# Issuing the later loads of a decode-step kernel from ACT's queue instead of POOL's

## The chip, the cores and the metric

The kernel runs on one core of one Trainium2 chip. A core has five engines with an instruction stream each: PE (matmul), DVE (VectorE), ACT (ScalarE), POOL (GpSimd) and SP (SyncE). Data moves between the device memory (HBM) and the on-chip memory (SBUF) by transfers (DMAs), which an engine issues with a `dma_start` in its own stream and which sixteen DMA engines carry out. A transfer adds to a semaphore sixteen times, once for each DMA engine that is through with its part; it has landed when all sixteen have come. The metric is the device time in microseconds.

## The reference

One decode step with its gradients: a layer norm of `x` (4 x 1 x 512), attention over the last 1024 of 4096 cached positions with 32 query heads on 8 key/value heads, and beside it a gated feed-forward part. The outputs are the result and the gradients by all inputs but one.

```
xn = _layernorm(x)
out = x + _A_ref(xn, k_cache, v_cache, wq, wo) + _B_ref(xn, w_gate, w_up, w_down)
...
W = min(4096, max(256, Sk // 4))                     # 1024
q = (x @ wq) as (B, Hq, Sq, Dh)
k = repeat(k_cache[:, :, Sk - W:, :], 4);  v likewise
p = softmax(q k^T * Dh ** -0.5);  o = p v;  return o @ wo
...
_B_ref: (gelu(x @ w_gate) * (x @ w_up)) @ w_down
```

The gradients by the caches (`out_2`, `out_3`) have the caches' full shape, 33.5 MB each: the last quarter of the positions is computed, the other three quarters are zeros that the kernel has to write.

## The kernel before

**Stages.** First the feed-forward part: `w_down`, `w_gate`, `w_up` are loaded, transposed, multiplied, and the outer products that give their gradients are put in a list `bg` of small pieces. Then comes attention in `NT` = 4 groups (`t` = 0 to 3) of `GP` = 2 key/value heads (`g`). For each group the loop at L766 runs `masks`, `scores(t, 0)` (transposes of K and the scores), `scores(t, 1)` (transposes of V, and the softmax by hooks), `softmax_d`, `pre(t + 1)` (the projections of the next group, with `wo` and `wq`), `odq`, `fin` (the sums that read `wo` and `wq` last), `load_next`, the rest of `bg`, and `dw`, which puts the weight gradients' pieces in `bg`.

**What `scores` does.** Eight steps: for each of the two heads `g` four blocks `q`. A step transposes eight 128 x 128 blocks (L402, `T_ps`, in one of the four buffers of the PSUM pool `ps_w`), copies them with DVE (`T_sb`, L101), multiplies (L407), and then calls `tick`, which takes one or two pieces from `bg`. A piece is a matmul into another buffer of `ps_w` and a copy out of it (`evac`), in most cases by ACT (L99), in some by DVE (L101). The last piece of a tile issues the store, always from SP (`store`, L105).

**The zeros.** `zeros(n)` issues stores of a constant zero tile `ztile` from ACT, 1.5 or 3 MB each (18 in all), in `scores` after block `q == 1` of each head, with numbers by the table `ZN`, and at some other places. `add_manual_dep` ties such a store to the last ACT copy made so far (`last[-1]`): it comes behind that copy in ACT's stream.

**The loads.** `load_w(t)` loads 1 MB of `wo` and 1 MB of `wq`, `load_kv(t, k, g)` 1 MB of K (`kb`, k = 0) or V (`vb`, k = 1). Group 0's, and K and V of group 1's first head, come from SP at the start. All later ones come from POOL: `wo`, `wq`, and K and V of group 1's second head when the feed-forward pools close (L763 to L765), and in `load_next(t)` those of group `t + 2`. There are sixteen of these. K and V have three buffers in `kvp` and one in `wodd`, the weights one in `wres` (even groups) and one in `wodd` (odd groups): a load waits until the group two before has read its tile for the last time. For K and V that is `odq`, for `wo` the sums at the end of `fin`.

**The order.** The order on each engine is fixed when the program is built, by a planner that goes by priority and modelled readiness. So POOL's loads don't stand in the order in which they are written: a V and a K load of group `t + 2` come ahead of the weights.

Of the kernel before, what the change touches and what calls it, by code (L numbers as in the profile page):

```python
# [13 lines left out]
BF16 = mybir.dt.bfloat16  # L14
P = 128
# [3 lines left out]
def kernel(  # L19
# [27 lines left out]
    nc = tc.nc  # L47

    B, Sq, D = A_x.shape
    _, G, Sk, Dh = A_k_cache.shape  # L50
# [4 lines left out]
    K0 = Sk - W  # L55
    F = B_w_gate.shape[1]
    ND = D // P
    NF = F // P
    MB = P // B
    J = W // MB  # L60
    GP = 2
    NT = G // GP
    HG = GP * rep
# [5 lines left out]
    CW = HG * Dh  # L69
# [18 lines left out]
    last = []  # L88
    chain = []

    def evac(out, in_, n, half=False, eng=None):

        eng = "dve" if half else eng or ("act" if chain else None)
        ca, cd = (190 + n) / 1.2, (120 + (n / 2 if half else n)) / 0.96
        if eng is None:
            eng = "act" if load["act"] + ca <= load["dve"] + cd else "dve"
        load[eng] += ca if eng == "act" else cd
        if eng == "act":
            last.append(nc.scalar.copy(out=out, in_=in_))  # L99
            return last[-1]  # L100
        return nc.vector.tensor_copy(out=out, in_=in_)  # L101
# [14 lines left out]
    for c0 in range(0, NF, NF // 2):  # L116
        nc.sync.dma_start(out=wd_sb[:, c0:c0 + NF // 2, :],
                          in_=B_w_down[c0 * P:(c0 + NF // 2) * P, :].rearrange("(c p) n -> p c n", p=P))
# [47 lines left out]
    for b in range(B):  # L166
        nc.vector.tensor_copy(out=sel[:, :, b * rep:(b + 1) * rep],
                              in_=ident_f[:, b * RB:b * RB + 1].unsqueeze(2).broadcast_to([P, 2 * GP, rep]))
# [69 lines left out]
    for src, dstT, adj in ((dy_b, dyT, False), (xn_b, xnT, True)):  # L238
# [4 lines left out]
        if src is dy_b:  # L243
# [3 lines left out]
                                  in_=tps[:].rearrange("p c (b r) -> p c b r", b=B)[:, :, :, 0:8])  # L247
# [22 lines left out]
    wo_v = A_wo.rearrange("(t p k) n -> t p k n", p=P, k=HG)  # L270
    wq_v = A_wq.rearrange("(p c) (t j) -> t p c j", p=P, j=CW)
    wo_t, wq_t, k_t, v_t = {}, {}, {}, {}
# [1 line left out]
    wpool = [wres]  # L274
    kvpool = [kvp] * 3

    def load_w(t):
        eng = nc.gpsimd if t else nc.sync
        pool = wpool[t % 2]
        wo_t[t] = pool.tile([P, HG, D], BF16, name="wo_sb", tag="wo")  # L280
        eng.dma_start(out=wo_t[t][:], in_=wo_v[t])
        wq_t[t] = pool.tile([P, ND, CW], BF16, name="wq_sb", tag="wq")
        eng.dma_start(out=wq_t[t][:], in_=wq_v[t])

    def load_kv(t, k, g):
        d_, src, nm = ((k_t, A_k_cache, "kb"), (v_t, A_v_cache, "vb"))[k]
        tl = kvpool[(GP * t + g) % (2 * GP)].tile([P, J, Dh], BF16, name=nm, tag=nm)
        (nc.gpsimd if GP * t + g > GP else nc.sync).dma_start(out=tl[:].rearrange("p j d -> p (j d)"),
                          in_=src[:, t * GP + g, K0:Sk, :].rearrange("b (m j) d -> m b (j d)", j=J))
        d_[(t, g)] = tl  # L290

    def load_next(t):

        if t + 2 < NT:
            load_w(t + 2)
            for k in range(2):
                for g in range(GP):
                    load_kv(t + 2, k, g)


    zruns = deque([og, 0] for og in (out_2, out_3))
# [21 lines left out]
    def tick(n):  # L323
        for _ in range(min(n, len(bg))):
            bg.popleft()()
# [67 lines left out]
    def scores(t, k, hooks):  # L393

        lf = (qm, dom)[k]
        blks = (k_t, v_t)[k]
        ps = ps_a.tile([P, WQ], FP32, name="S_ps", tag=("S", "dP")[k])
        for g in range(GP):
            for q in range(NQ):
                T_ps = ps_w.tile([P, JQ, P], BF16, name="T_ps", tag="w")  # L400
                for jj in range(JQ):
                    nc.tensor.transpose(T_ps[:, jj, :], blks[(t, g)][:, q * JQ + jj, :], ident[:])  # L402
                T_sb = tsb.tile([P, WQ, B], BF16, name="T_sb", tag="T", bufs=4)
                evac(T_sb[:].rearrange("p n b -> p (n b)"), T_ps[:].rearrange("p j m -> p (j m)"), 1024, half=True)
                s = q * GP + g
                for b in range(B):
                    nc.tensor.matmul(ps[b * RG:(b + 1) * RG, :], lhsT=lf[:, b, s * RG:(s + 1) * RG],  # L407
                                     rhs=T_sb[:, :, b], start=(g == 0 and q == 0),
                                     stop=(g == GP - 1 and q == NQ - 1), tile_position=(0, b * RG))
                for f in hooks.get(g * NQ + q, ()):  # L410
                    f()
                tick(2 if k or q % 2 else 1)
                if q == 1:
                    zeros(ZN[t][GP * k + g])
        st[t][("S", "dP")[k]] = ps[:]
# [195 lines left out]


    NF4 = (NF + 3) // 4
    load_w(0)
    for k in range(2):
        for g in range(GP):
            load_kv(0, k, g)
    for k in range(2):
        load_kv(1, k, 0)
# [106 lines left out]
    for f4 in range(NF4):  # L726
        held = {}
        n = min(4, NF - 4 * f4)
# [30 lines left out]
    with tc.tile_pool(name="stage", bufs=4, reuse_waits="tile") as stage, \  # L759
            tc.tile_pool(name="wodd", bufs=1, reuse_waits="tile") as wodd:  # L760
        wpool.append(wodd)
        kvpool.append(wodd)
        load_w(1)  # L763
        for k in range(2):
            load_kv(1, k, 1)  # L765
        for t in range(NT):  # L766
            if t == 0:
                pre(t, {})
            masks(t)
            scores(t, 0, {})  # L770
            zeros(2 if t == 0 else 0)
            scores(t, 1, softmax(t))
            d1, d2 = softmax_d(t)
            zeros(4 if t == NT - 1 else 0)
            if t + 1 < NT:
                pre(t + 1, {0: [d1], 2: [d2]})
            else:
                tick(2)
                d1()
                tick(6)  # L780
                d2()
                tick(2)
            odq(t)
            fin(t)
            load_next(t)
            tick(len(bg))
            dw(t)
        tick(len(bg))
        zeros(2 * B * G)


        acc_r = kvp.tile([P, 2, ND, B, RB], FP32, name="acc_r", tag="kb")
        nc.vector.tensor_copy(out=acc_r[:], in_=acc[:].unsqueeze(4).broadcast_to([P, 2, ND, B, RB]))
        fin_ps = []
        for o in range(2):
            f_ps = ps_w.tile([P, ND, P], FP32, name="f_ps", tag="w")
            for c in range(ND):
                nc.tensor.transpose(f_ps[:, c, :], acc_r[:, o, c].rearrange("p b r -> p (b r)"), ident_f[:])
            fin_ps.append(f_ps[:])
        acc_o, acc_d = fin_ps[0].rearrange("p c d -> p (c d)"), fin_ps[1].rearrange("p c d -> p d c")  # L800

        def adj(x):
            return x[:].rearrange("p (d c) -> p d c", c=ND)

        out_b = kvp.tile([P, D], BF16, name="out_b", tag="vb")
        nc.vector.tensor_tensor(out=out_b[:], in0=acc_o, in1=x_b[:], op=ALU.add)
        nc.sync.dma_start(out=out_0.rearrange("b s d -> (b s) d"), in_=out_b[0:P:RB, :])

        s1 = const.tile([P, 1], FP32, name="s1")
        nc.vector.reduce_sum(out=s1[:], in_=acc_d, axis=AX.XY)  # L810
        pr = kvp.tile([P, D], FP32, name="pr", tag="vb")
        s2 = const.tile([P, 1], FP32, name="s2")
        nc.vector.tensor_tensor_reduce(out=adj(pr), in0=acc_d, in1=adj(xn_f), scale=1.0, scalar=0.0,
                                       op0=ALU.mult, op1=ALU.add, accum_out=s2[:])
        nm1 = const.tile([P, 1], FP32, name="nm1")
        nc.vector.tensor_scalar(out=nm1[:], in0=s1[:], scalar1=-1.0 / D, scalar2=None, op0=ALU.mult)
        nm2 = const.tile([P, 1], FP32, name="nm2")
        nc.vector.tensor_scalar(out=nm2[:], in0=s2[:], scalar1=-1.0 / D, scalar2=None, op0=ALU.mult)
        nc.vector.scalar_tensor_tensor(out=adj(pr), in0=adj(xn_f), scalar=nm2[:, 0:1], in1=acc_d,
                                       op0=ALU.mult, op1=ALU.add)  # L820
        nc.vector.tensor_scalar(out=pr[:], in0=pr[:], scalar1=nm1[:, 0:1], scalar2=rstd[:, 0:1],
                                op0=ALU.add, op1=ALU.mult)
        dx_b = kvp.tile([P, D], BF16, name="dx_b", tag="kb")
        nc.vector.tensor_tensor(out=dx_b[:], in0=pr[:], in1=dy_b[:], op=ALU.add)
        nc.sync.dma_start(out=out_1.rearrange("b s d -> (b s) d"), in_=dx_b[0:P:RB, :])
# [30 lines left out]
```

## Time and profile before

| | us |
|---|---|
| median of 3 runs | 281.89 (280.82 to 281.97) |
| the profiled execution's own time | 281.41 |
| its span, first to last instruction | 279.6 |

| engine | busy | share of the span | instructions |
|---|---|---|---|
| PE | 212.1 us | 76% | 3126 |
| DVE | 158.7 us | 57% | 336 |
| ACT | 115.0 us | 41% | 214 |
| POOL | 56.0 us | 20% | 56 |

HBM was read for 30.68 MB and written for 81.01 MB. Issues of transfers are not counted in an engine's busy time. In the profile a `q` behind an engine's name (ACTq) is its sequencer, which waits and issues; q1 is the queue that SP's transfers go through, q10 ACT's, q0 POOL's. What POOL issued around the ends of groups 0 and 1:

| issued at, us | transfer | idle before it |
|---|---|---|
| 42.15, 42.89, 43.66, 44.18 | wo, wq, kb, vb of group 1 | 21.31 us for the pieces of the feed-forward part |
| 97.18, 99.63 | vb, kb of group 2 | |
| 104.22, 104.74, 105.49, 106.02 | wo, wq, kb, vb of group 2 | 3.99 us for the sums of `fin` |
| 149.98, 152.44 | vb, kb of group 3 | |
| 156.47, 156.99, 157.75, 158.27 | wo, wq, kb, vb of group 3 | 3.44 us for the sums of `fin` |

### The profile page before, as it was taken

To read this page: it belongs to the slowest core of one execution; us is meant where nothing else is said; L and a number is where in the kernel's file an instruction comes from. 1 tells how busy PE (TensorE), PEld (TensorE's weight loads), DVE (VectorE), ACT (ScalarE), POOL (GpSimd) and SP (SyncE) were. 2 spreads that over 40 slices of the span, in tenths; PEclk is the share of its full clock that TensorE was granted. 3 is DMA by queue.
4 is the path that set the end of the run, shared out by engine and by line. 5 is a ranking of instruction groups with operands and counts; after the bars stand their busy time and mean duration, and the time that the engine had idled before them with its cause. 6 is when DMAs were issued, how large, how long until landed. Compare 5 with 4: busy or idle time off the path is not lost.

```text
span 279.6 us, 7185 instructions
## 1 busy us (share of the span) xinstructions
PE 212.1 (76%) x3126; PEld 137.7 (49%) x3132; DVE 158.7 (57%) x336; ACT 115.0 (41%) x214; POOL 56.0 (20%) x56
## 2 busy tenths in 40 slices
PE   1978976988769879968797978699897775689400
PEld 0856854744435565535465745356664442355200
DVE  6955644546357657654665555477654634376530
ACT  1331643444335246636253544373444442525400
POOL 3890003040200345020007600200520020020000
PEclk9985998699797997999689999999999997597955
DMA  7999999999999999999999999999999999999970
GB/s 236 446 392 430 425 403 392 414 411 423 425 426 422 422 423 416 417 432 423 427 418 350 387 407 430 421 425 421 425 415 431 428 422 423 425 432 421 422 311 22
DMA packets 19423, 112.15 MB, mean 401 GB/s; under 512 B 1456, under 2 KB 5056, under 8 KB 10432
## 3 DMA queue, kind: packets, MB, share of 16 engines
q10 hardware_dynamic: 4400, 50.34, 42.7%
q1 hardware_dynamic: 12304, 44.58, 39.3%
q0 software_dynamic: 2688, 16.78, 15.0%
q8 instruction: 24, 0.39, 0.5%
q14 instruction: 7, 0.06, 0.0%
HBM read 30.68 MB, written 81.01 MB: 399 GB/s over the span
## 4 chain that ended last, share of the span: by engine, by line
PE 52%; DVE 19%; DMA 18%; issue 3%; POOL 2%; ACT 2%; ACTq 0%; DVEq 0%
DMA out_dram<-osb_q 13%; PE T_ps L402 9%; PE kv_ps L540 8%; DVE T_sb L101 6%; PE S_ps L407 6%; DMA out_dram<-osb_g 5%; PE woT_ps L339 3%; PE wgT_ps L745 3%; PE acc_ps L213 2%; PE wqT_ps L598 2%; PE dwo_ps L559 2%; POOL P_x L420 2%; PE od_ps L512 2%; PE dwg_ps L718 2%; PE do_ps L344 2%
## 5 line engine op out<-in xcount | busy, mean ns | idle before, releaser
L101 DVE COPY T_sb<-T_ps 128x1024 bf16<-128x1024 bf16 x64 | 43.8, 690 | 40.1 <-PE T_ps L402 39.6
L99 ACT CAST stg_dv<-kv_ps 128x512 bf16<-128x512 f32 x57 | 30.1, 594 | 33.5 <-PE kv_ps L540 25.8
L99 ACT CAST stg_dk<-kv_ps 128x512 bf16<-128x512 f32 x40 | 22.3, 592 | 36.4 <-PE kv_ps L540 22.8
L540 PE MATMUL kv_ps<-domr,P_x 128*128 128x512 bf16 x63 | 23.4, 439 | 10.5 <-ACT stg_dv L99 5.1
L387 POOL TENSOR_TENSOR domr<-r,msk 128x512 bf16<-128x512 bf16 x8 | 8.2, 1040 | 74.1 <-DVE r L380 74.1
L99 ACT CAST osb_g<-dwg_ps 128x512 bf16<-128x512 f32 (+1 forms) x28 | 14.2, 538 | 19.0 <-PE dwg_ps L718 9.2
L402 PE MATMUL T_ps<-ident,kb 128*128 128x128 bf16 x256 | 21.9, 222 | 0.0
L402 PEld LDWEIGHTS <-kb 128*128 128x128 bf16 x256 | 17.1, 100 | 8.6 <-issue 5.7
L540 PE MATMUL kv_ps<-qmr,dS_x 128*128 128x512 bf16 x60 | 20.9, 432 | 0.5 <-DVE stg_dk L101 0.2
L402 PE MATMUL T_ps<-ident,vb 128*128 128x128 bf16 x256 | 20.8, 223 | 0.1
L99 ACT CAST osb_o<-dwo_ps 128x512 bf16<-128x512 f32 x25 | 14.6, 586 | 12.9 <-PE dwo_ps L559 11.8
L402 PEld LDWEIGHTS <-vb 128*128 128x128 bf16 x256 | 16.2, 100 | 6.9 <-issue 5.0
L407 PE MATMUL S_ps<-T_sb,dom 128*32 128x256 bf16 x128 | 12.7, 387 | 8.3 <-DVE T_sb L101 7.8
L420 POOL TENSOR_TENSOR P_x<-P_b,bmsk 128x1024 bf16<-128x1024 bf16 x4 | 7.6, 1893 | 56.2 <-ACT P_b L468 56.2
L99 ACT CAST osb_q<-dwq_ps 128x512 bf16<-128x512 f32 x25 | 14.1, 589 | 11.1 <-PE dwq_ps L571 6.1
L101 DVE CAST stg_dk<-kv_ps 128x512 bf16<-128x512 f32 x24 | 16.0, 684 | 1.8 <-PE kv_ps L540 1.7
L101 DVE COPY woT<-woT_ps 128x1024 bf16<-128x1024 bf16 x16 | 11.0, 689 | 10.0 <-PE woT_ps L339 10.0
L407 PE MATMUL S_ps<-T_sb,qm 128*32 128x256 bf16 x128 | 13.1, 388 | 4.0 <-DVE T_sb L101 4.0
L339 PE MATMUL woT_ps<-ident,wo_sb 128*128 128x128 bf16 x128 | 12.3, 248 | 2.7 <-DVE stg_dv L101 1.9
L101 DVE COPY wgT<-wgT_ps 128x1024 bf16<-128x1024 bf16 x14 | 9.7, 692 | 7.6 <-PE wgT_ps L745 7.6
L339 PEld LDWEIGHTS <-wo_sb 128*128 128x128 bf16 x128 | 10.4, 113 | 7.2 <-issue 6.4
L101 DVE COPY wqT<-wqT_ps 128x1024 bf16<-128x1024 bf16 x16 | 11.0, 687 | 4.7 <-PE wqT_ps L598 4.6
(214 smaller groups left out, 397.4 us busy)
## 6 DMA issues: line engine op xcount, KB each, us to landing
out_dram<-ztile ACTq DMA_DIRECT2D x14, 3072.0 KB, 22.4
out_dram<-stg_dv SPq DMA_DIRECT2D x8, 1024.0 KB, 25.4
out_dram<-stg_dk SPq DMA_DIRECT2D x8, 1024.0 KB, 17.2
out_dram<-ztile ACTq DMA_DIRECT2D x4, 1536.0 KB, 12.7
kb<-in_A_k_cache_dram POOLq DMA_DIRECT2D x5, 1024.0 KB, 20.0
vb<-in_A_v_cache_dram POOLq DMA_DIRECT2D x5, 1024.0 KB, 24.3
out_dram<-osb_o SPq DMA_DIRECT2D x8, 512.0 KB, 15.8
out_dram<-osb_q SPq DMA_DIRECT2D x8, 512.0 KB, 28.1
```

The costliest lines, as they stand in the source:

```text
L99: last.append(nc.scalar.copy(out=out, in_=in_))
L101: return nc.vector.tensor_copy(out=out, in_=in_)
L213: nc.tensor.matmul(ps[:, c, :], lhsT=lf(c), rhs=rhs, start=(k == 0), stop=(k == len(terms) - 1))
L339: nc.tensor.transpose(wT_ps[:, i, c, :], wo_sb[:, 2 * h2 + i, c * P:(c + 1) * P], ident[:])
L344: nc.tensor.matmul(do_ps[i * RG:(i + 1) * RG, 2 * h2:2 * h2 + 2], lhsT=dyT8[:, c, :], rhs=woT[:, :, c, :].rearrange("p j (g x) -> p j g x" ...
L387: nc.gpsimd.tensor_tensor(out=mr[:, g], in0=st[t]["r4"][:, k, :].unsqueeze(1).broadcast_to([P, NQ, Dh]), in1=msk[:, :, g].unsqueeze(2).bro ...
L402: nc.tensor.transpose(T_ps[:, jj, :], blks[(t, g)][:, q * JQ + jj, :], ident[:])
L407: nc.tensor.matmul(ps[b * RG:(b + 1) * RG, :], lhsT=lf[:, b, s * RG:(s + 1) * RG], rhs=T_sb[:, :, b], start=(g == 0 and q == 0), stop=(g = ...
L420: eng.tensor_tensor(out=dst[:].rearrange("p j (m b) -> p (j m) b", b=B), in0=src[:].unsqueeze(2).broadcast_to([P, WQ, B]), in1=bmsk[:].uns ...
L512: nc.tensor.matmul(od_ps[r0:r0 + rep * B, 0, :], lhsT=pT[:, j % JQ, (j // JQ) * GP + g:P:NS], rhs=blks[(t, g)][:, j, :], start=(j == 0), s ...
L540: nc.tensor.matmul(mps[:].rearrange("p q d -> p (q d)"), lhsT=src[:, jj, :], rhs=mr[:, g].rearrange("p q d -> p (q d)"), start=True, stop= ...
L745: nc.tensor.transpose(wT_ps[:, i, c, :], wsb[:, c, fc * P:(fc + 1) * P], ident[:])
```

## The change

Every load that POOL issued is now issued by ACT. Each is tied to the last ACT copy made so far, as the zeros are. For groups 2 and 3 the two weight tiles are loaded at once in `load_next`, when a group ends. K and V of those groups are put in a list `loads`, as are all four later loads of group 1. `pull(1)` takes one from the list, in `scores(t, 0)`, after the blocks `q` = 0 and 2 of each head: four per group, in the order in which they were put in. For group 1 that is `wo`, `wq`, K, V during group 0's K steps; for groups 2 and 3 the two K and then the two V tiles, during the K steps of groups 1 and 2.

```diff
@@ -274,28 +274,42 @@
-    def load_w(t):
-        eng = nc.gpsimd if t else nc.sync
+    loads = deque()
+
+    def pull(n):
+        for _ in range(min(n, len(loads))):
+            loads.popleft()()
+
+    def fetch(out, in_, first):
+        d = (nc.sync if first else nc.scalar).dma_start(out=out, in_=in_)
+        if not first:
+            tc.add_manual_dep(d.ins, last[-1].ins.name,
+                              mybir.DependencyInfo(mybir.DependencyClass.NoSync, mybir.DependencyReason.DATA))
+
+    def load_w(t, k):
         pool = wpool[t % 2]
-        wo_t[t] = pool.tile([P, HG, D], BF16, name="wo_sb", tag="wo")
-        eng.dma_start(out=wo_t[t][:], in_=wo_v[t])
-        wq_t[t] = pool.tile([P, ND, CW], BF16, name="wq_sb", tag="wq")
-        eng.dma_start(out=wq_t[t][:], in_=wq_v[t])
+        if k == 0:
+            wo_t[t] = pool.tile([P, HG, D], BF16, name="wo_sb", tag="wo")
+            fetch(wo_t[t][:], wo_v[t], t == 0)
+        else:
+            wq_t[t] = pool.tile([P, ND, CW], BF16, name="wq_sb", tag="wq")
+            fetch(wq_t[t][:], wq_v[t], t == 0)
 
     def load_kv(t, k, g):
...
-        (nc.gpsimd if GP * t + g > GP else nc.sync).dma_start(out=tl[:].rearrange("p j d -> p (j d)"),
-                          in_=src[:, t * GP + g, K0:Sk, :].rearrange("b (m j) d -> m b (j d)", j=J))
+        fetch(tl[:].rearrange("p j d -> p (j d)"),
+             src[:, t * GP + g, K0:Sk, :].rearrange("b (m j) d -> m b (j d)", j=J), GP * t + g <= GP)
         d_[(t, g)] = tl
 
     def load_next(t):
 
         if t + 2 < NT:
-            load_w(t + 2)
+            for k in range(2):
+                load_w(t + 2, k)
             for k in range(2):
                 for g in range(GP):
-                    load_kv(t + 2, k, g)
+                    loads.append(lambda k=k, g=g: load_kv(t + 2, k, g))
@@ -410,6 +424,8 @@
                 tick(2 if k or q % 2 else 1)
+                if k == 0 and q % 2 == 0:
+                    pull(1)
                 if q == 1:
                     zeros(ZN[t][GP * k + g])
@@ -760,9 +777,10 @@
-        load_w(1)
         for k in range(2):
-            load_kv(1, k, 1)
+            loads.append(lambda k=k: load_w(1, k))
+        for k in range(2):
+            loads.append(lambda k=k: load_kv(1, k, 1))
```

More of the change, by code (lines that the diff above doesn't have):

```diff
@@ L613 @@
     NF4 = (NF + 3) // 4
-    load_w(0)
+    for k in range(2):
+        load_w(0, k)
     for k in range(2):
@@ L762 @@
         kvpool.append(wodd)
-        load_w(1)
         for k in range(2):
-            load_kv(1, k, 1)
+            loads.append(lambda k=k: load_w(1, k))
+        for k in range(2):
+            loads.append(lambda k=k: load_kv(1, k, 1))
         for t in range(NT):
```

## The prediction

> **What bounds the kernel now.** I read the slices over time first, then the queues.
>
> ```profile
> DMA  7999999999999999999999999999999999999970
> GB/s 236 446 392 430 425 403 392 414 411 423 425 426 422 422 423 416 417 432 423 427 418 350 387 407 430 421 425 421 425 415 431 428 422 423 425 432 421 422 311 22
> ...
> q10 hardware_dynamic: 4400, 50.34, 42.7%
> q1 hardware_dynamic: 12304, 44.58, 39.3%
> q0 software_dynamic: 2688, 16.78, 15.0%
> q8 instruction: 24, 0.39, 0.5%
> ```
>
> The transfers are full from the second slice to the last but two, at about 425 GB/s. 112.15 MB at 425 GB/s is 264 us of the 279.6 us span, while TensorE, the busiest engine, has 76%. So a change of queue pays only through the bytes per second, holes in the stream, or the tail. q0 is POOL's queue: the 16.78 MB that the change moves. q10 is ACT's (the zero stores), q1 is SP's. Next, the same by stretch:
>
> ```profile
> core 0: us, PE busy (x) PEld busy (x) DVE busy (x) ACT busy (x) POOL busy (x), PEclk, DMA share, GB/s
> 138.00:149.00 11.00, 10.58 (x252) 7.15 (x250) 7.61 (x15) 4.74 (x10) 1.00 (x1) 0.82 1.01 420
> 150.00:157.00 7.00, 5.54 (x104) 4.29 (x104) 3.54 (x7) 3.71 (x7) 3.55 (x6) 1.00 0.95 322
> 208.00:256.00 48.00, 35.77 (x462) 20.97 (x461) 25.07 (x48) 19.32 (x38) 3.79 (x2) 0.88 1.01 425
> 272.00:278.00 6.00, 0.00 (x0) 0.00 (x0) 0.00 (x0) 0.00 (x0) 0.00 (x0) 0.50 0.08 33
> ```
>
> Two rows matter. In 272 to 278 the share is 0.08, little more than one of sixteen DMA engines: fifteen are through, one drags out the end. The semaphore records agree: of the sixteen increments of the last osb_q store, half are in by 271.4 us and the last comes at 278.45, **7 us late**. In 150 to 157 only 322 GB/s flow although the engines count as busy; 8192-byte packets of q0 there take 464 ns on average, the usual one 309. For wo's third load (issued 156.5), fourteen increments come by 166.9 us, the last two at 172.2 and 173.8: two engines fell behind on POOL's loads.
>
> The chain of waits shows what the late engine does upstream:
>
> ```profile
> 226.83 35.79 DMA out_dram<-osb_q
> ...
> 262.71 0.59 ACT osb_q L99
> ```
>
> The last is what an ACT-issued transfer can cost, in ACT's timeline:
>
> ```profile
> 233.69 0.61 ACTq L105 DMA_DIRECT2D out_dram<-ztile  x1
> 234.34 1.56 ACT L99 CAST stg_dv<-kv_ps 128x512 bf16<-128x512 f32 x3 [4.38 <-DMA out_dram<-stg_dk]
> ```
>
> A zero store reads a constant tile, yet it waited for a stg_dk store. By its semaphores, SP and ACT draw their transfers from one cycle of eight semaphores, and each waits for the landing of the one eight before it; POOL has eight of its own. The copy behind waited 4.38 us.
>
> **What the Trainium skill says.** "DMA: Bandwidth & Descriptors", section "Issuing engines are not separate DMA queues": all issuers use the same 16 engines, a change of issuer saves only sequencer time. The trace agrees on the whole: a share per MB of 0.85% (q10), 0.88% (q1), 0.89% (q0). The same page, "Latency and other measured facts": two engines (7 and 15) are usually slower, with the descriptor ring of GpSimd's transfers in SBUF as a best guess. Two late engines on POOL's loads fit; the cause isn't shown. "Queues, rings and completion order": each engine takes packets by turns from the queues, and in order within one. That fits the 35.79 us of a 512 KB osb_q store (2048-byte packets against 12288-byte zero packets). It means that loads on ACT's queue stand behind the zeros before them.
>
> **The change part by part.**
>
> *Removed: POOL's issue.* Sixteen transfers at 0.53 to 0.77 us, some 10 us of an engine with 20% busy and waits of 74.1 us for r and 56.2 us for P_b. Worth nothing.
>
> *Added: ACT's issue.* The same sixteen at ACT's own 0.61 us (zero stores): 10 us, ten of them before 157 us (wo, wq, K, V of group 1; wo, wq, two K, two V of group 2). ACT is 41% busy, but its copies free the four ps_w buffers that the transposes need. If a third of the six us of the ten reaches TensorE: +2 us; bounds 0 and +6. The six of group 3 come after 157 us, where 35.79 us of the chain is waiting for a transfer: nothing. The release of wo (last read by acc_sum) doesn't block: it held POOL until 104.22 us, when ACT was idle 2.88 us for a kv_ps anyway.
>
> *Moved: group 1's loads, from 42 us to the K steps at 52 to 64 us.* Zero and FFN stores carry the stream until about 52 us: from 42 to 56.9 us they have some 4.2 MB, 9.9 us at 425 GB/s. Then the loads come one per two K steps. A hole of up to 2 us. In return the osb_d and osb_g stores of 40 to 57 us meet no loads at first and land earlier; ACT waits 7.0 us for osb_g and 2.2 us for osb_d landings. A third of that 9.2 us on the path: -3 us; bounds 0 and -7.
>
> *Moved: K and V of group 3, from 149.98 and 152.44 us to after 157 us.* This is the clear price. In 150 to 157 us, 7 x 322 = 2.25 MB moved, of which 1.02 MB were these two loads by the packet records. The rest is 1.2 MB, 2.9 us at 425: **4.1 us of hole**. Now the same 7 us hold 2.25 / 0.425 = 5.3 us of work, so 1.7 us are lost already. Net +2.4 us. What the stream gains or loses before 150 us is swallowed there, since the queues are nearly dry at 149 us; only the pace of compute shifts it. With +2 and -3 from above: **+1.4 us at 157 us**.
>
> *Order on the queue.* Group 3's last V load stands behind 2 MB of weights, three other MB and 4.6 MB of zeros; 10.7 MB at some 300 GB/s is 36 us from 156 us, landing about 192 us. It lands at 201.36 us now, and is needed about 221 us. No reader waits.
>
> *The eight semaphores.* A group of 51 us now has about 12 SP and ACT transfers; with loads 18. Eight in flight allow 8 x 51 / 18 = 22 us each, and zeros take 22.4 us. Walking the order eight back, I find no binding wait before 150 us and two or three of some 4 us in group 2, in front of a load or a zero store. They hold ACT's copies, then ps_w, then TensorE. The 35.79 us hide them; costed 0, bounds 0 and +6 (if they come before 157 us).
>
> *The late engine.* Between the first transfers and POOL's first (36 to 44 us) the last engine is 1.6 to 3.3 us behind; after POOL's loads 5 to 9, and 7 at the end. Without a software queue I take 3 us: **-4 us**; bounds 0 (it has another cause) and -7 (it goes). What is late next is the fifteen engines themselves, at about 271.5 us.
>
> Sum: 1.4 - 4.0 = -2.6 us on the profiled run's own 281.41 us (span 279.6 and 1.8 around it): 278.8 us. The median of the runs shown is 281.89, 0.5 above; I say **279.0 us**.
>
> **Rivals.**
> *The late engine stays* (chance 0.21). It comes from instruction fetches (24 packets, some 22 us of engine time, on whichever engine) or from reads. For: wide gaps in 195 to 207 us with few loads left. Against: the step at 150 to 165 us. Then +1.4: about 283.
> *ACT is blocked* (0.33), slower: load and wait stand in ACT's order in groups 0 and 1, where the stream depends on compute. The place is the ps_w copies behind a load; the price, ten loads at 1.2 us (issue and half a microsecond of wait), half on the path, 6 us in place of the 2, without the -3: hole 2.4 + 6, less half the tail gain, 2: about 287.5. It decides once stalls before 157 us pass 2.6 us beyond what I took. For: the 4.38 us above. Against: in groups 0 and 1 zeros wait little today.
> *All of the lag goes* (0.10): also the 35.79 us shrink, the end is at the fifteen engines' 271.5 plus 1.8 and a little: about 274.5.
> That nothing changes because all issuers share the engines is the first rival with its hole filled.
>
> **How the numbers follow.** Forecast case 0.36, 276 to 280.5 us. A difference under 0.5% (1.4 us) can't be told from none here. Faster: 0.33 of the forecast, 0.10 full gain, 0.02 of the first rival: 0.45. Same: 0.03 and 0.12: 0.15. Slower: 0.07 and 0.33: 0.40. Range 274 to 288: it leaves out half of the full gain and the upper part of the blocked case.
>
> **What would show it.** q0 gone, ACT's queue at 67.1 MB; the stretch 272 to 278 empty or short and the last increments within 3 us; a dip in the GB/s near 150 us; ACT's waits for landings in front of loads few before 150 us. Wrong if the last 7 us still run at one engine's rate, or if TensorE waits for ACT in 50 to 150 us by more than 5 us over now.

## The result, and the profile after

| | before | after |
|---|---|---|
| median | 281.93 us (280.82 to 282.18, 4 runs) | 289.96 us (289.10 to 292.25, 4 runs) |
| ratio | | 1.0305, interval 1.0234 to 1.0376 |
| the profiled execution's own time, its span | 281.41, 279.6 us | 292.25, 290.3 us |

The kernel became 3% slower, where 279.0 us had been forecast. The profiled execution is the slowest of the four: the traces differ by 10.7 us, the medians by 8.0. Of runs 4 and 5 below, one execution each was in a slower state and is left out of their medians and ratios; run 4's trace is of it. The page of the changed kernel, slices over time and queues:

```profile
DMA  7999999999999969999997499999999999999991
GB/s 243 443 397 423 419 410 425 343 360 431 421 430 419 426 191 375 413 418 423 419 429 303 162 306 424 420 429 420 423 427 422 425 426 421 432 417 426 426 411 73
...
q10 hardware_dynamic: 7856, 67.12, 56.7%
q1 hardware_dynamic: 12304, 44.58, 37.9%
```

q0 is gone and ACT's queue has its 16.78 MB: the change does what it says. But the GB/s now have three holes where there was one shallow dip, and in two of them even the busy share of the DMA engines falls. The same stretches by time, first the kernel before, then the changed one:

```profile
core 0: us, PE busy (x) PEld busy (x) DVE busy (x) ACT busy (x) POOL busy (x), PEclk, DMA share, GB/s
48.00:64.00 16.00, 14.89 (x189) 9.39 (x189) 8.56 (x18) 7.37 (x15) 4.04 (x4) 0.84 1.01 410
96.00:112.00 16.00, 13.62 (x169) 8.59 (x170) 9.87 (x19) 7.89 (x14) 8.62 (x11) 0.89 1.00 418
150.00:176.00 26.00, 21.34 (x270) 13.78 (x269) 14.81 (x28) 13.21 (x25) 7.77 (x11) 1.00 1.00 393
```

```profile
48.00:64.00 16.00, 13.85 (x180) 9.17 (x180) 7.50 (x15) 7.03 (x14) 4.03 (x4) 0.85 0.96 359
96.00:112.00 16.00, 11.86 (x199) 7.88 (x201) 7.11 (x15) 4.96 (x9) 3.89 (x3) 0.75 0.81 292
150.00:176.00 26.00, 23.11 (x434) 15.70 (x433) 16.64 (x31) 12.37 (x24) 5.92 (x5) 0.96 0.77 284
```

What is missing after, counted at 425 GB/s: 16 x 51 / 425 = 1.9 us, 16 x 126 / 425 = 4.7 us and 26 x 109 / 425 = 6.7 us, 13.3 in all. At the end 2.3 us come back: the last increment of the last store is 4.7 us behind the median one, where it was 7.0. That leaves 11.0 us, near the 10.7 us between the spans.

The largest hole comes because the compute that makes the bytes runs slower, the first one from the late loads (runs 6 and 7 will show both). The chain that ended last, by engine, before and after:

```profile
PE 52%; DVE 19%; DMA 18%; issue 3%; POOL 2%; ACT 2%; ACTq 0%; DVEq 0%
```

```profile
PE 60%; DVE 26%; issue 4%; ACT 2%; POOL 2%; DVEq 0%; ACTq 0%
```

The 18% of DMA are gone: 86% of the changed kernel's chain are TensorE and DVE. The granted clock isn't the reason: it was 0.888 and 0.885 over the two spans. Start times of each group's K steps (first transpose of K), worked out from the trace, show where:

| | K of group 0 | 1 | 2 | 3 | last transpose of wq, group 3 |
|---|---|---|---|---|---|
| before | 52.0 | 107.9 | 157.3 | 204.6 | 250.7 us |
| after | 52.0 | 112.9 | 167.6 | 220.3 | 261.6 us |

Groups 0, 1 and 2 are 5.0, 5.3 and 5.4 us longer each, and group 3 is 4.8 us shorter: no transfer is left in the chain, where there was one of 35.79 us. Of the 15.7 us that the three groups lost, 11.6 lie in their K steps (from the first transpose of K to the first of V). They are just the groups in whose K steps a load is taken from the list. But TensorE doesn't wait for a load there. What it waited for (in total, times, longest), before and after:

```profile
PE S_ps L407 <- DVE T_sb L101: 11.8, 28, 0.8
```

```profile
PE S_ps L421 <- DVE T_sb L101: 19.9, 38, 0.8
```

Eight more microseconds of score matmuls waiting for the copy of a transposed block. ACT hardly waited for landings in the changed kernel:

```profile
ACT stg_dv L99 <- remote: 2.5, 1, 2.5
...
ACT osb_g L99 <- DMA out_dram<-osb_d: 0.7, 1, 0.7
```

Before, it had waited 7.0 us for osb_g stores, 4.4, 3.4, 2.6 and 2.2 us for others. TensorE's timeline in the K steps of group 1 shows what changed (start, duration, tiles; an idle stretch before it and who ended it in brackets; DVE's copies of the same time behind the dots), before and after:

```profile
113.67 0.61 PE L402 MATMUL T_ps<-ident,kb 128*128 128x128 bf16 x8
114.11 0.39 PE L559 MATMUL dwo_ps<-dyz,od_x 128*128 128x512 bf16 x1
114.43 0.40 PE L407 MATMUL S_ps<-T_sb,qm 128*32 128x256 bf16 x4
114.76 0.41 PE L571 MATMUL dwq_ps<-od_x,xnz 128*128 128x512 bf16 x1
115.00 0.39 PE L402 MATMUL T_ps<-ident,kb 128*128 128x128 bf16 x4
...
113.64 1.36 DVE L101 COPY T_sb<-T_ps 128x1024 bf16<-128x1024 bf16 x2 [1.11 <-PE T_ps L402]
```

```profile
118.79 0.61 PE L416 MATMUL T_ps<-ident,kb 128*128 128x128 bf16 x8
119.24 0.39 PE L575 MATMUL dwo_ps<-dyz,od_x 128*128 128x512 bf16 x1
120.19 0.40 PE L421 MATMUL S_ps<-T_sb,qm 128*32 128x256 bf16 x4 [0.56 <-DVE T_sb L101]
120.51 0.62 PE L416 MATMUL T_ps<-ident,kb 128*128 128x128 bf16 x8
121.92 0.40 PE L421 MATMUL S_ps<-T_sb,qm 128*32 128x256 bf16 x4 [0.78 <-DVE T_sb L101]
...
119.44 0.69 DVE L101 COPY T_sb<-T_ps 128x1024 bf16<-128x1024 bf16 x1 [1.34 <-PE T_ps L416]
121.17 0.69 DVE L101 COPY T_sb<-T_ps 128x1024 bf16<-128x1024 bf16 x1 [1.04 <-PE T_ps L416]
```

Before, the next block's transposes are under way while DVE copies the last one. After, transposes, copy and scores of one block follow each other, and TensorE stands idle for most or all of the copy (0.69 us). The planner put TensorE's work in another order, and it gave the tiles other buffers. Here are the buffers of `ps_w` (0 to 3) of the work tiles in group 1's K steps, in the order of the program, T for T_ps, o and q for the pieces `dwo_ps` and `dwq_ps`:

```
before  T3 o2 T1 o0 o3 T2 o1 T0 o3 o2 T1 o0 T3 o2 q1 T0 q3 T2 q1 q0
after   T2 o0 T3 o1 o2 T0 o3 T2 o0 o2 T1 o3 T1 o1 q0 T2 q3 T2 q2 q1
```

Before, the four go round, three other tiles between two users of one. After, T1 o3 T1 and T2 q3 T2 occur: the second block can't be transposed before DVE has copied the first. Counted over the K and V steps and their pieces, 23, 25 and 34% of the tiles of groups 0, 1 and 2 have their buffer's last user one or two places ahead in the changed kernel, against 10, 6 and 16% before. In group 3 the two kernels have the same share.

### The profile page after: what moved, and what is told of

Read it like the earlier page. It is cut to its first block, busy times and chain, and to the rows that moved or that the text cites. A ratio compares the mean times of both kernels' runs of the same rounds, so it can differ in the third digit from the quotient of the medians.

```text
span 290.3 us, 7161 instructions
## 1 busy us (share of the span) xinstructions
PE 216.2 (74%) x3126; PEld 142.2 (49%) x3132; DVE 159.7 (55%) x336; ACT 114.8 (40%) x214; POOL 46.4 (16%) x40
## 4 chain that ended last, share of the span: by engine, by line
PE 60%; DVE 26%; issue 4%; ACT 2%; POOL 2%; DVEq 0%; ACTq 0%
PE T_ps L416 11%; PE kv_ps L556 10%; DVE T_sb L101 10%; PE S_ps L421 8%; PE woT_ps L353 3%; PE acc_ps L213 3%; PE dwo_ps L575 3%; PE wgT_ps L762 3%; PE od_ps L528 3%; PE wqT_ps L614 2%; PE dwg_ps L735 2%; POOL P_x L436 2%; DVE stg_dk L101 2%; PE do_ps L358 1%; PE pT_ps L447 1%
## 5 line engine op out<-in xcount | busy, mean ns | idle before, releaser
L556 PE MATMUL kv_ps<-qmr,dS_x 128*128 128x512 bf16 x60 | 21.5, 439 | 3.7 <-DVE dS_x L436 1.4
L416 PE MATMUL T_ps<-ident,vb 128*128 128x128 bf16 x256 | 22.0, 231 | 0.0
L99 ACT CAST osb_g<-dwg_ps 128x512 bf16<-128x512 f32 (+1 forms) x28 | 14.2, 537 | 19.8 <-PE dwg_ps L735 19.0
L421 PE MATMUL S_ps<-T_sb,qm 128*32 128x256 bf16 x128 | 13.1, 387 | 11.5 <-DVE T_sb L101 11.3
L416 PEld LDWEIGHTS <-kb 128*128 128x128 bf16 x256 | 17.9, 105 | 7.1 <-issue 4.6
L416 PEld LDWEIGHTS <-vb 128*128 128x128 bf16 x256 | 17.7, 104 | 6.5 <-issue 3.6
L421 PEld LDWEIGHTS <-qm 128*32 128x32 bf16 x128 | 5.3, 93 | 17.9 <-issue 15.9
```

Source lines behind the costliest of these rows:

```text
L556: nc.tensor.matmul(mps[:].rearrange("p q d -> p (q d)"), lhsT=src[:, jj, :], rhs=mr[:, g].rearrange("p q d -> p (q d)"), start=True, stop= ...
```

## The experiments

Two theories stood after the traces. **The loads**: taken late, and one by one, behind ACT's copies, they leave holes in the stream or hold ACT up. **The planner**: the change made it choose another order and other buffers, and the loads themselves cost little. All ratios are to the kernel before on the same chip.

**1. Late, but from POOL.** The loads are put off as in the change, but POOL issues them; each really waits for the ACT copy. TensorE's order and the buffers are those of the kernel before.

```diff
     def fetch(out, in_, first):
-        d = (nc.sync if first else nc.scalar).dma_start(out=out, in_=in_)
+        d = (nc.sync if first else nc.gpsimd).dma_start(out=out, in_=in_)
...
-                              mybir.DependencyInfo(mybir.DependencyClass.NoSync, mybir.DependencyReason.DATA))
+                              mybir.DependencyInfo(mybir.DependencyClass.Sync, mybir.DependencyReason.DATA))
```

> The changed kernel with its later loads issued by POOL again, at the changed places: each load waits for the ACT copy that it is tied to. The order on TensorE, VectorE and ACT is that of the kernel before. Theory 'late loads' (K and V are held to the K steps, the transfers run dry at the ends of groups 0 and 1): the holes near 104 and 158 us are there, 287 to 291 us. Theory 'ACT in the way' (the issue on ACT and the other order of matmuls slow compute by 5 us a group): no slowing of compute, 281 to 284 us. Half of each: 285.

Measured: 283.77 us (7 runs), 1.0067 (1.0044 to 1.0089). Late loads alone cost 2 us of the 8. The first K step comes at 50.3 us and group 0 ends 5.1 us earlier (96.2 against 101.3 us), as the prediction had hoped from freed stores, and none of it is left at the end.

**2. From ACT, but at once.** ACT issues, but nothing is put off: `load_w` and `load_kv` are called where they stood before.

```diff
-                    loads.append(lambda k=k, g=g: load_kv(t + 2, k, g))
+                    load_kv(t + 2, k, g)
...
-            loads.append(lambda k=k: load_w(1, k))
+            load_w(1, k)
...
-            loads.append(lambda k=k: load_kv(1, k, 1))
+            load_kv(1, k, 1)
```

> The changed kernel with ACT as issuer, but nothing put off: all six loads of a group in load_next, group 1's four where the feed-forward pools close. Late loads: the holes go, 280 to 283 us. ACT in the way: ten loads before 157 us still stand in ACT's order, 286 to 290 us. The late engine of the prediction's forecast: if POOL's queue was its cause, the last increments come within 3 us of the median and the time is below 280.

Measured: 284.39 us (5 runs), 1.0087 (1.0053 to 1.0122). Here ACT is held up once: K of group 2, issued at 106.04 us, stood in front of copies, and the way from group 0's last wq transpose to the next K step took 11.5 us in place of 6.6. That is the prediction's rival "ACT is blocked", but in this kernel, not in the changed one. The planner chose a little differently here: TensorE's order differs from the old one in 49 of 3120 places, and the buffers are another set, with nearly the same distances (for 15 of the 392 tiles the last user is nearer or farther).

**3. ACT's issue time alone.** The kernel before, with twelve loads of 256 bytes by ACT where the change has its loads. They draw from the same semaphores, and go to a tile (`xn_b`) that nothing reads any more.

```diff
                 tick(2 if k or q % 2 else 1)
+                if k == 0 and q % 2 == 0 and t + 1 < NT:
+                    small(t, 2 * g + q // 2)
```

> The kernel before with POOL's loads as they were, and twelve loads of 256 bytes from ACT at the places where the change puts its pulled loads (into a tile that nothing reads any more). It prices the issue on ACT and the draw on the eight semaphores alone. ACT in the way by its issue time: 284 to 288 us. Late loads, or an order that follows from large loads: 281 to 283 us.

Measured: 281.41 us (20 runs), 0.9999 (0.9985 to 1.0012). The issues cost nothing. This left the sum of the parts, 2 us for late and 2.5 for ACT, well short of 8, while run 1 had the old order and buffers, and runs 2 and 3 came close to both (in run 3, 5 places of the order and 12 distances differ).

**4 and 5. TensorE's order, exchanged.** To hold an order, the end of the program ties each matmul and transpose to the one that is to stand ahead of it; the tie is one of order alone (`NoSync`). ACT's copies and activations are tied in the same way, but their order is the same in every kernel here. Once the changed kernel gets the old order, once the kernel before gets the new one.

```diff
+        for runs, seen in ((_PE, t_seen),):
+            want = [seen[i] for a, n in runs for i in range(a, a + n)]
...
+            for p, q in zip(want, want[1:]):
+                tc.add_manual_dep(q.ins, p.ins.name,
+                                  mybir.DependencyInfo(mybir.DependencyClass.NoSync, mybir.DependencyReason.DATA))
```

> The changed kernel with TensorE's order of instructions held to that of the kernel before (3126 matmuls and transposes); the loads keep their places in ACT's stream and their late times. Theory 1 (the loss is the new order that the planner gave TensorE: transposes and score matmuls of the K steps in series, 5.3 us in each of groups 0 to 2): the three K phases go back from 14 to 16 us to 10 to 12 us, the time to 282 to 285 us. Theory 2 (the loss is made by ACT as issuer together with late loads, by holes in the stream, and the order only mirrors it): 288 to 291 us, K phases still 14 us or more.

> The kernel before, its loads on POOL and at their old times, with TensorE's order held to that of the changed kernel. Theory 1 (the order): groups 0 to 2 are some 3 to 5 us longer each, the time 286 to 291 us, though no load is late. Theory 2 (late loads on ACT): 281 to 283 us, as the kernel before.

Measured: the changed kernel with the old order 288.30 us (3 runs), 1.0266 (1.0222 to 1.0311); the kernel before with the new order 289.69 us (3 runs), 1.0267 (1.0223 to 1.0311). The second says that the order alone can cost what the change cost, with no load moved; the first, that the old order doesn't mend it. So the theory of the order alone fell. In the first run the waits had not gone but moved: dwo matmuls now waited 0.8 us for a T_sb copy, which they don't read. They could only wait for its buffer. This is where the buffers came in. (The second run had neither the old buffers nor the changed kernel's: the planner made a third set, in which 4 of the 392 distances differ from the old ones. DVE's order goes with TensorE's.)

**6, 7 and 8. Order and buffers.** In place of one pool of four buffers there are four pools of one, and a table gives each of the 392 tiles its pool; the order is held as well.

```diff
-    ps_w = ctx.enter_context(tc.tile_pool(name="ps_w", bufs=4, space=bass.MemoryType.PSUM))
+    ps_w4 = [ctx.enter_context(tc.tile_pool(name=f"ps_w{i}", bufs=1, space=bass.MemoryType.PSUM)) for i in range(4)]
+    ps_w = _Fixed(ps_w4)
...
+    def tile(self, *a, **k):
+        self._n += 1
+        return self._pools[int(_BUF[self._n - 1])].tile(*a, **k)
```

The changed kernel with order and buffers of the kernel before:

> The changed kernel with both choices of the planner held to those of the kernel before: TensorE's order, and which of the four ps_w buffers each of the 392 work tiles gets. The loads keep the issuer, the places and the times of the change. Theory 1 (the loss is in the planner's other choices, buffers and order together: with the changed kernel's buffers and the old order a dwo matmul still waited 0.8 us for a T_sb copy): the K phases go back to 9 to 12 us, the waits on T_sb are gone, the time is 282 to 285 us. Theory 2 (the loss is in late loads on ACT's queue): 288 to 291 us as in the changed kernel.

The kernel before with both of the changed kernel's, and with the buffers alone:

> The kernel before, loads on POOL at their old times, with the changed kernel's order on TensorE and its ps_w buffers. Theory 1 (planner's choices): K phases of 14 to 16 us in groups 0 to 2, 286 to 290 us. Theory 2 (late loads on ACT's queue): 281 to 283 us.

> The kernel before with the changed kernel's ps_w buffers alone; TensorE's order stays. If a tile's buffer alone can put a matmul behind a T_sb copy, waits of PE on T_sb appear as in the run with the old order (0.6 and 0.8 us per step) and the time is 285 to 290 us; if the order does it all, 281 to 283 us.

| | median | ratio |
|---|---|---|
| the change, old order and buffers | 283.69 us (5 runs) | 1.0078 (1.0047 to 1.0108) |
| before, new order and buffers | 292.91 us (4 runs) | 1.0409 (1.0367 to 1.0452) |
| before, new buffers only | 289.00 us (4 runs) | 1.0253 (1.0208 to 1.0297) |

This settles it. The planner's choices without the loads cost as much as the whole change, or more; the loads without the planner's choices cost a quarter of it. That the tables and ties themselves cost nothing is seen in run 12, which has them too and is level with the kernel before. What TensorE waited for in the first two, the total first:

```profile
PE S_ps L28 <- DVE T_sb L140: 11.2, 26, 0.8
```

```profile
PE S_ps L28 <- DVE T_sb L140: 19.8, 37, 0.8
```

11.2 is the kernel before (11.8), 19.8 is the changed kernel (19.9). And in the third, where the order was the old one and the buffers were not:

```profile
PE S_ps L28 <- DVE T_sb L140: 10.1, 24, 0.8
...
PE T_ps L28 <- DVE T_sb L140: 3.2, 6, 0.6
PE dwq_ps L28 <- DVE T_sb L140: 3.1, 4, 0.8
PE dwg_ps L28 <- DVE T_sb L140: 2.8, 5, 0.8
...
PE dwo_ps L28 <- DVE T_sb L140: 1.6, 2, 0.8
```

The last four read no T_sb. 10.7 us are waits for a buffer; they stand in the timeline like this:

```profile
117.20 0.61 PE L28 MATMUL T_ps<-ident,kb 128*128 128x128 bf16 x8 [0.55 <-DVE T_sb L140]
118.59 0.38 PE L28 MATMUL dwo_ps<-dyz,od_x 128*128 128x512 bf16 x1 [0.78 <-DVE T_sb L140]
```

The new order doesn't make up for these buffers. In the kernel before it costs 3.9 us on top of them (292.91 against 289.00 us), and in the changed kernel the two orders can't be told apart (1.0305 and 1.0266, whose intervals overlap). With distances like the old ones the new order is a loss by itself, 2.7% (run 5).

The holes split too. In the three stretches run 6 has 350, 412 and 381 GB/s, run 7 has 413, 414 and 234. So the hole of 48 to 64 us is that of the late loads, the one of 150 to 176 us mostly that of order and buffers, and the one of 96 to 112 us (292 in the changed kernel) appears only when both come together.

**9. The buffers in turn.** If reuse too soon is the cause, it needn't be the old set: the changed kernel with the old order, tile `i` in buffer `i` mod 4.

```diff
-        return self._pools[int(_BUF[self._n - 1])].tile(*a, **k)
+        return self._pools[(self._n - 1) % 4].tile(*a, **k)
```

> The changed kernel with TensorE's order of the kernel before, and the four ps_w buffers given out strictly in turn (tile i gets buffer i mod 4), so that every work tile has three others between it and the last user of its buffer. In the changed kernel 23 to 34% of the K and V steps' tiles of groups 0 to 2 follow the last user of their buffer at a distance of one or two, in the kernel before 6 to 16%. Theory 1 (reuse too soon is what makes matmuls wait for a T_sb copy): 282 to 285 us, as with the buffers of the kernel before. Theory 2 (only the exact set of buffers of the kernel before is good, by some other property): 287 us or more.

Measured: 283.32 us (4 runs), 1.0064 (1.0042 to 1.0085). A set of buffers that neither kernel had is as good as the old one. So with the old order the distance counts, and not the exact set. That far-apart buffers alone would do, with the new order left, isn't shown; run 5 speaks against it.

**10. The 2 us that are left.** The changed kernel with old order and buffers, but the put-off loads all at the first K step of a group.

```diff
-                if k == 0 and q % 2 == 0:
-                    pull(1)
+                if k == 0 and g == 0 and q == 0:
+                    pull(4)
```

> The changed kernel with order and buffers of the kernel before, and the put-off loads all issued behind the first K step of a group instead of one by one over four. Theory 1 (the 2.0 us that were left with old order and buffers are the holes in the stream at 54 to 60 and 158 to 166 us, made by loads that come singly and late): the holes shrink, 281.5 to 283 us. Theory 2 (they come from something else, the late engine at the end or ACT's waits): 283.5 to 285 us.

Measured: 283.48 us (8 runs), 1.0066 (1.0045 to 1.0087): no gain that can be told. The hole of 48 to 64 us shrank (380 GB/s, in run 6 350, before 410), but that of 150 to 176 us grew (330, in run 6 381, before 393).

**11 and 12. Parts that could have paid.** In one, POOL issues all and only group 1's loads are put off (held as in run 1); in the other, only group 3's six loads go to ACT, at once, with order and buffers held (the edit of this one is shown).

```diff
-        eng = nc.gpsimd if t else nc.sync
+        eng = nc.scalar if t == 3 else nc.gpsimd if t else nc.sync
...
-        (nc.gpsimd if GP * t + g > GP else nc.sync).dma_start(out=tl[:].rearrange("p j d -> p (j d)"),
+        (nc.scalar if t == 3 else nc.gpsimd if GP * t + g > GP else nc.sync).dma_start(out=tl[:].rearrange("p j d -> p (j d)"),
```

> POOL stays the issuer; only the four loads of group 1 are put off to the K steps of group 0, held behind the ACT copy; groups 2 and 3 load as in the kernel before. In the run with all loads held on POOL group 0 ended 5.1 us earlier (96.2 against 101.3 us), and groups 1 and 2 lost it. Theory A (putting off group 1's loads frees the stores of the feed-forward part and the gain lasts): 277 to 280 us. Theory B (the transfers bound the end, so that an earlier end of group 0 is only waited off later): 281 to 283 us.

> The kernel before, order and buffers held to its own, with the six loads of group 3 alone issued by ACT where load_next stands; groups 1 and 2 stay on POOL. If the late engine at the end comes from POOL's last loads, the lag of 7 us goes to 5 us or less as in the changed kernel and the time is 278.5 to 280.5 us. If ACT is held up by the loads that wait for their tiles at 150 to 158 us, or the lag stays, 281 to 284 us.

Measured: 283.52 us (8 runs), 1.0083 (1.0056 to 1.0111), and 281.81 us (14 runs), 1.0010 (0.9989 to 1.0030). In the first, K steps start 5.2 us earlier in group 1, but the stream loses 16 x 71 / 425 = 2.7 us in 48 to 64 us (339 GB/s), wins back 26 x 30 / 425 = 1.8 us in 150 to 176 us (423), and the last increment comes 8.6 us late instead of 7.0: theory A fell. In the second the last increment comes 8.1 us late, not earlier. No kernel of this study beat the one before.

## Why the prediction was wrong, by its own steps

**What bounds the kernel**: right for the kernel before. That what the stream gains before 150 us is swallowed there held too: runs 1 and 11 start group 1's K steps 5 us earlier and end no earlier. But full transfers were taken for a property that the change would keep. In the changed kernel no DMA is left in the chain.

**The step that failed: the pace of compute, with order and buffers taken as unchanged.** The prediction says that "only the pace of compute shifts it", and prices that pace at +2 - 3 = -1 us before 157 us. Measured were +5.0, +5.3 and +5.4 us in groups 0, 1 and 2. The prediction prices added, removed and moved transfers one by one and takes, without a reason, TensorE's order and the buffers of `ps_w` as they were, though a planner sets both each time the program is built. It looked at ACT's copies, which free those buffers; the waits that grew were for DVE's. Of the 3.05%, 0.78% are left when order and buffers are held to the old ones, so about 2.3%, 6.4 us, are the planner's. (The parts don't add up: with no load moved the same order and buffers cost 4.1%.) No term of the sum stands for it.

**ACT's issue**, +2 us with bounds 0 and +6: for small loads it measured 0 (run 3). Real loads can also make ACT wait, for which see the next term.

**The eight semaphores**, 0: right for the changed kernel, where ACT's waits for landings fell to 0.7 us, with 2.5 us more of a remote wait. The bound of +6 was the right sort of caution. With the loads at once (run 2) the wait came, and in run 6 twice, as the prediction had walked it: ACT stood 4.0 us in front of the V load of 118.31 us, whose semaphore had last served the wo load of 101.92 us, and 4.4 us in front of the zero store of 177.41 us, whose semaphore had served that of 159.63 us. Both lie on the chain of run 6. What they cost in the time isn't shown: its group 2 is 5.4 us longer than in the kernel before, its group 3 4.9 us shorter.

**The rival "ACT is blocked"** gave 287.5 us, near the measured time, by luck: its reason is not what happened. Its own test was TensorE waiting for ACT in 50 to 150 us by over 5 us more. That wait went from 1.1 us to nothing; the wait for DVE grew from 10.8 to 17.7 us. ACT's timeline in group 1's K steps shows the loads issued beside copies, with each copy waiting for its matmul:

```profile
114.42 0.59 ACT L99 CAST osb_o<-dwo_ps 128x512 bf16<-128x512 f32 x1 [0.69 <-PE dwo_ps L575]
114.42 0.60 ACTq L284 DMA_DIRECT2D kb<-in_A_k_cache_dram  x1
115.16 0.58 ACT L99 CAST osb_o<-dwo_ps 128x512 bf16<-128x512 f32 x1 [0.16 <-PE dwo_ps L575]
116.96 0.58 ACT L99 CAST osb_o<-dwo_ps 128x512 bf16<-128x512 f32 x1 [1.22 <-PE dwo_ps L575]
116.97 0.55 ACTq L284 DMA_DIRECT2D kb<-in_A_k_cache_dram  x1
```

**Group 1's loads moved**, a hole of up to 2 us and -3 in return: with order and buffers held (run 6) the hole is 16 x 60 / 425 = 2.3 us. The return is real in the pace (runs 1, 6 and 11 have group 1's K steps 3 to 5.6 us earlier) and worth nothing in the time.

**K and V of group 3**, a hole of 4.1 us, net +2.4: run 6 shows the stretch of 150 to 176 us at 381 against 393 GB/s, 26 x 12 / 425 = 0.7 us more than before.

**The late engine**, -4 us with bounds 0 and -7: the changed kernel's -2.3 lies within the bounds, but by luck, since the cause was wrong. In run 6, with nothing on POOL, the last increment is 7.2 us behind, in run 12 8.1; in run 7, with all the loads on POOL, 3.0. It goes with the holes, not with the queue: below. (The sum's last step is off as well: 281.89 less 2.6 is 279.3, not 279.0.)

**What stays open.** Runs 1, 6, 9 and 10 agree on some 2 us for loads that come late, whoever issues them. Run 11 puts off group 1's loads alone and costs as much, so the hole that these leave in 48 to 64 us, 2.3 to 2.7 us, is the likeliest source. In run 6 the stream is some 0.55 MB, 1.3 us, behind that of the kernel before at 272 us, by the holes less what other stretches made up; I have not split the rest. Run 10 shifted the holes and didn't lessen their cost. The change with its new order and the old buffers wasn't run, so the share of each of the two in it is open. Why the planner chose other buffers wasn't tried either: the twelve tiny loads also moved it to another set, one that does no harm.

## What to carry to other kernels

Where a planner sets the order and hands out the buffers, a small change in one engine's stream can reorder another engine that it doesn't touch: compare the two orders and the buffers of each tile before you reason about the change itself, and hold both fixed to measure the change alone. If matmuls wait for a copy that they don't read, look at who had their buffer last; handing the four out in turn, with the old order held, mended most of it here. This kernel's transfers were full, and still it was bound by compute once three groups took a tenth longer: price a loss of pace in every group, not only in the one where the stream has a dip.

## What the runs showed of the hardware that was not expected

**After a hole in the stream the last DMA engine lags less.** The last increments of the final stores, behind the median one, beside the rate in 150 to 176 us:

| kernel | GB/s in 150 to 176 us | last increment late by |
|---|---|---|
| 12, group 3's loads from ACT | 409 | 8.1 us |
| before, loads from POOL | 393 | 7.0 us |
| 6, all from ACT, old order and buffers | 381 | 7.2 us |
| 10, all from ACT, first K step | 330 | 4.7 us |
| after, all from ACT | 284 | 4.7 us |
| 7, all from POOL, new order and buffers | 234 | 3.0 us |

The runs that are left out fit in: run 11 (POOL) has 423 GB/s and 8.6 us, run 1 (POOL) 386 and 6.2, run 9 (ACT) 385 and 7.4, run 3 (POOL) 382 and 6.7, run 2 (ACT) 318 and 4.7, run 8 (POOL) 287 and 5.4, run 5 (POOL) 257 and 3.0. In the changed kernel the lag is 1.7 us at 158 us and 0.1 us at 167 us, after the hole, and comes to 4.8 at the end. That would fit one engine that is a little slower than its fifteen fellows, with a lag that adds up while the stream is full. It stays an inference: the records don't number the engines, and the lag of single stores goes up and down in between (1.2 to 14.2 us after 200 us in the kernel before). The page "DMA: Bandwidth & Descriptors" of the Trainium skill, "Latency and other measured facts", offers the descriptor ring of GpSimd's transfers as a best guess for slower engines. Here the lag is as large without any such transfer: in run 6, with nothing on POOL's queue, the DMA share from 275 to 281 us is 0.07, one engine of sixteen.

**Buffers of PSUM.** The page "Perfetto Trace Analysis" of the Trainium skill, "Matmuls", says that independent groups of matmuls should rotate through different banks, so that the copy of one overlaps the next. The trace agrees, and puts a price on it: where the rotation is broken by a T_ps tile, the next user waits 0.5 to 0.8 us on average, 17 times and 10.7 us in all in run 8.
